# Two paddings that move the start addresses of an FFN's matmul operands

## The chip, the cores and the metric

The kernel runs on one core of a Trainium2 chip. The metric is device microseconds of one execution of the program, lower is better. Three executions of the kernel before took 951.02, 951.64 and 956.59 us; the median is 951.64 us.

## The reference

A conditioned block with two halves on 2048 tokens of 640 channels, all in float32:

```python
mod = (_silu(c) @ w_mod).reshape(c.shape[0], 6, 1, -1)          # sa, ca, ga, sb, cb, gb
h = _layernorm(x) * (1 + ca) + sa
x = x + ga * _A_ref(h, ...)      # a long convolution (S4D): a kernel K is generated from
                                 # exponentials and sines, and applied by FFT over 4096 points
h = _layernorm(x) * (1 + cb) + sb
gate = einsum("bsd,df->bsf", h, w1); up = einsum("bsd,df->bsf", h, w3)      # F = 1728
x = x + gb * einsum("bsf,fd->bsd", _silu(gate) * up, w2)
```

## The kernel before, in words

The program has two stages. The first (up to about 380 us) makes the convolution: five blocks of 128 channels each; GpSimd, VectorE and ScalarE generate phases, sines and products (tiles `ph`, `xx`, `yy`), and TensorE turns these into the convolution's kernel (`kps`) and applies the transforms (`ps`, `fh`, `fk`, `fz`). Its order is written out by hand in a table of task numbers. TensorE's operands here are plain float32, and one such matmul shows as two records in the trace.

The second stage (from about 380 us to the end) is the FFN, on four blocks of 512 tokens, in two passes of two blocks each. Each float32 operand is split into a high and a low part of type float32r (function `split`: the high part is a copy that rounds, the low part the rest), and a product of two such numbers is three matmuls: high by high, high by low, low by high (function `three`). Every one of these has a stationary operand of 128x128 and a moving operand of 128x512. The two up projections of two blocks are combined in a scheme with seven products in place of eight (function `group`): per tile of 128 hidden channels 54 matmuls, over 11 tiles in the first pass and 13 in the second. A tile of the down projection (function `down`) is 15 matmuls, 5 output tiles times three; the last half tile of 64 has 10. A few tiles run in a plain form.

Where the operands lie matters for this change. Stationary operands of the FFN are the split weights `wh`, `wl` (pool `wp`, function `pair`) and `w` (the down weights, function `w2_tile`). Moving operands are the split activations `x0h` to `x8l`, `ah`, `al` and the sums `T` (pool `fp`, functions `x_new`, `hidden_split`). Pools without a side are laid out from the low addresses of a partition upwards, in the order in which they are opened: `const` first, then `x0`, and in the second stage `xp` and `wp`. Pools on the right are laid out down from the high end: `core`, and in the second stage `fp`. Within a pool tiles follow each other. So padding in `const` moves up everything in the pools without a side that is opened after it, and padding late in `fp` moves down all tiles of `fp` made before it.

The scheduler of the second stage and the hand-written order of the first are not touched, and neither looks at addresses. Program order is the same on every engine in both kernels, instruction by instruction.

Of the kernel before, what the change touches and what calls it, by code (L numbers as in the profile page):

```python
# [10 lines left out]
F32 = mybir.dt.float32  # L11
# [7 lines left out]
P = 128  # L19
# [186 lines left out]
class K:  # L206
# [18 lines left out]
    def setup(self):  # L225
        nc = self.nc
        c = self.const = self.pool("const")
        self.ident = c.tile([P, P], F32, name="ident")
        make_identity(nc, self.ident)
        self.hpi = c.tile([P, 1], F32, name="hpi")  # L230
        nc.gpsimd.memset(self.hpi, HPI)
        self.ones = c.tile([P, 1], F32, name="ones")
        nc.gpsimd.memset(self.ones, 1.0)
        self.cols = c.tile([P, 3, KT], F32, name="cols")
        c.tile([P, 32], F32, name="pad")
        d = self.dram = self.pool("dram", space=DRAM)
        self.hs = d.tile([NB, 4, 4, 32, 4, P], F32, name="hs")
        self.zd = d.tile([32, 2, 64, D], F32, name="zd")
        self.w2d = d.tile([14, P, 2, D], F32, name="w2d")
        self.xv = self.x.rearrange("(t1 q j) d -> q t1 j d", t1=32, q=4, j=NJ)  # L240
        self.ov = self.out.rearrange("(t1 q j) d -> q t1 j d", t1=32, q=4, j=NJ)
# [1104 lines left out]
    def ffn(self):  # L1346

        W, X, v, w2 = self.first
        for b in (2, 3):
            self.load_x2(b)  # L1350
        pend = self.groups(0, range(2, 13), X, self.acc, W[2], (w2[2][:, 0], w2[2][:, 1]), None)
        acc, X, W, w2, pend = self.late(0, self.acc, pend)
        pend = self.groups(1, range(13), X, acc, W, w2, pend)
        self.late(1, acc, pend)
# [762 lines left out]
```

## Time and profile before

| what | value |
|---|---|
| median of three runs | 951.64 us (951.02 to 956.59) |
| profiled execution: span from first to last instruction | 950.6 us (no other time is recorded for it) |
| PE busy | 868.3 us (91%), 8369 matmul records |
| weight loads (PEld) busy | 686.4 us (72%) |
| VectorE (DVE) busy | 684.2 us (72%) |
| ScalarE (ACT) busy | 549.9 us (58%) |
| GpSimd (POOL) busy | 342.1 us (36%) |
| mean granted TensorE clock | 0.984 |

PE is TensorE's matmuls and PEld its weight loads, which overlap them. A matmul's record is longer than its share of the stream, because matmuls are pipelined and their ends are modelled: 392 ns for one that starts about 229 ns after the one before. What counts is therefore the distance between the starts, here called the cadence, and not the record's length. L151 is the line of a helper that records instructions in order, so that tiles tell groups apart, not lines. Names of tiles are written out<-in, the moving operand first.

### The profile page before, as it was taken

The page shows a single profiled execution, that of the slowest core. Times are in us where ns is not written, and L with a number is a line of the kernel's source. Part 1 is how long each engine was busy: PE and PEld are TensorE (multiplying, and loading weights), DVE is VectorE, ACT ScalarE, POOL GpSimd, SP SyncE. Part 2 cuts the span into 40 slices and gives each one's busy share as a digit, 9 for nine tenths or more (in the row PEclk, how much of TensorE's full clock was granted, in tenths as well). Part 3 has the DMA queues.
Part 4 walks back from the last instruction along what each step waited for, and adds up shares of the span by engine and source line. Part 5 has one row for each costly group of instructions (what it writes and reads, how often), then busy time and mean ns, then how long its engine had stood idle before and what let it go on. Part 6 is the DMA issues. An engine that isn't in the chain of part 4 may idle for free.

```text
span 950.6 us, 21218 instructions
## 1 busy us (share of the span) xinstructions
PE 868.3 (91%) x8369; PEld 686.4 (72%) x8369; DVE 684.2 (72%) x1294; ACT 549.9 (58%) x1035; POOL 342.1 (36%) x371
## 2 busy tenths in 40 slices
PE   1267999999999986999999999999999999999997
PEld 0035858777888863787777778888788888888775
DVE  7997999999989878896776775657556555555422
ACT  6688999989797732754444444544444444443412
POOL 0899989998998500011111211000121212120000
PEclk9997999999999997999999999999999999999999
DMA  9976553524143598654533422375432222221374
GB/s 201 266 225 171 158 150 107 138 80 127 47 119 84 143 241 209 170 175 149 154 113 121 139 67 87 94 238 171 126 92 83 83 84 83 84 84 31 111 230 127
DMA packets 110508, 127.42 MB, mean 134 GB/s; under 512 B 10568, under 2 KB 90696, under 8 KB 109128
## 3 DMA queue, kind: packets, MB, share of 16 engines
q1 hardware_dynamic: 109032, 125.27, 46.7%
q8 instruction: 66, 1.08, 0.5%
q10 hardware_dynamic: 1376, 0.79, 0.3%
q14 instruction: 34, 0.28, 0.1%
HBM read 95.89 MB, written 30.15 MB: 133 GB/s over the span
## 4 chain that ended last, share of the span: by engine, by line
PE 73%; DVE 9%; ACT 8%; DMA 5%; issue 2%; POOL 1%; SPq 1%; ACTq 0%; DVEq 0%; POOLq 0%
PE c L151 19%; PE acc L151 18%; PE X L151 12%; PE ps L151 5%; PE kps L151 4%; PE fz L151 4%; PE fk L151 3%; PE fh L151 3%; PE gu L151 2%; ACT tr L151 1%; DVE xb L151 1%; PE iy L151 1%; DMA sp<-zd 1%; DMA zd<-zt 1%; DVE yy L151 1%
## 5 line engine op out<-in xcount | busy, mean ns | idle before, releaser
L151 PE MATMUL acc<-ah,w 128*128 128x512 f32 x560 | 173.4, 395 | 1.9 <-DMA w<-w2d 1.2
L151 PEld LDWEIGHTS acc<-ah,w 128*128 128x128 f32 x560 | 103.8, 188 | 25.3 <-ACT ah L598 1.8
L151 PE MATMUL acc<-al,w 128*128 128x512 f32 x260 | 102.3, 393 | 0.0
L599 DVE TENSOR_TENSOR wl<-s,wh 128x256 fp32r<-128x256 f32 x92 | 39.0, 424 | 67.0 <-ACT wh L598 66.5
L775 POOL TENSOR_TENSOR s<-wr 128x256 f32<-128x256 f32 x22 | 16.4, 743 | 184.8 <-DMA wr<-in_w 104.7
L598 ACT ACTIVATE wh<-s 128x256 fp32r<-128x256 f32 x92 | 37.6, 409 | 78.0 <-PE X L151 58.1
L151 POOL TENSOR_TENSOR ph<-p,p 128x1024 int32<-128x1024 int32 x40 | 78.8, 1970 | 6.2 <-ACT tr L151 5.6
L598 ACT ACTIVATE wh<-wr 128x256 fp32r<-128x256 f32 x92 | 38.4, 418 | 56.1 <-PE X L151 42.4
L776 POOL TENSOR_TENSOR s<-s,wr 128x256 f32<-128x256 f32 x22 | 17.1, 776 | 131.5 <-issue 128.0
L151 DVE TENSOR_TENSOR yy<-yy,tr 128x512 f32<-128x512 f32 (+1 forms) x60 | 56.5, 944 | 2.9 <-ACT tr L151 2.1
L836 ACT ACTIVATE t<-g 128x512 f32<-128x512 f32 x44 | 27.8, 632 | 52.9 <-DVE g L800 52.9
L151 PEld LDWEIGHTS acc<-al,w 128*128 128x128 f32 x260 | 48.9, 188 | 11.3 <-DVE al L599 0.4
L151 ACT ACTIVATE tr<-ph,hpi 128x512 f32<-128x512 f32 x80 | 54.5, 688 | 3.3 <-DVE yy L151 1.3
L151 DVE TENSOR_TENSOR xx<-tr,xx 128x512 f32<-128x512 f32 x80 | 54.2, 681 | 2.9 <-ACT tr L151 2.5
L805 DVE SCALAR_TENSOR_TENSOR g<-t,g 128x512 f32<-128x512 f32 x48 | 33.7, 701 | 31.3 <-ACT t L836 29.3
L151 PE MATMUL kps<-yy,xx 128*32 128x64 f32 x1920 | 37.8, 231 | 18.3 <-DVE xx L151 14.2
L151 PE MATMUL fz<-fp,wz 64*128 64x512 f32 x224 | 54.0, 608 | 0.3 <-DVE fp L151 0.3
L151 PEld LDWEIGHTS kps<-yy,xx 128*32 128x32 f32 x1920 | 32.8, 114 | 27.1 <-issue 11.1
L599 DVE TENSOR_TENSOR wl<-wr,wh 128x256 fp32r<-128x256 f32 x92 | 40.2, 438 | 15.1 <-ACT wh L598 15.0
L151 PE MATMUL ps<-wk,xb 128*64 128x128 f32 x640 | 47.2, 294 | 2.8 <-DVE hb L151 1.1
L151 ACT ACTIVATE tr<-ph 128x512 f32<-128x512 int32 x80 | 47.2, 599 | 2.3 <-DVE yy L151 1.8
L598 ACT ACTIVATE ah<-h 128x512 fp32r<-128x512 f32 x26 | 16.4, 632 | 53.1 <-PE acc L151 53.1
(454 smaller groups left out, 2442.3 us busy)
## 6 DMA issues: line engine op xcount, KB each, us to landing
w<-w2d SPq DMA_DIRECT2D x42, 640.0 KB, 3.9
wr<-in_w SPq DMA_DIRECT2D x50, 320.0 KB, 3.9
zd<-zt SPq DMA_DIRECT2D x40, 256.0 KB, 3.2
w2d<-w SPq DMA_DIRECT2D x14, 640.0 KB, 3.5
xs<-in_x SPq DMA_DIRECT2D x16, 320.0 KB, 11.9
hs<-hb SPq DMA_DIRECT2D x20, 256.0 KB, 3.2
xb<-hs SPq DMA_DIRECT2D x20, 256.0 KB, 4.8
iz<-zd SPq DMA_DIRECT2D x32, 160.0 KB, 4.2
```

The costliest lines, as they stand in the source:

```text
L151: self.prev = self.k.order(f(*a, **kw), self.prev)
L598: self.nc.scalar.activation(H, v, AF.Copy)
L599: eng.tensor_tensor(Lo, v, H.bitcast(F32), op=ALU.subtract)
L775: eng.tensor_tensor(s[0], u[:, 0:2], u[:, 2:4], op=ALU.add)
L776: eng.tensor_tensor(s[1], s[0], g[:, 0:2], op=ALU.subtract)
L805: V.scalar_tensor_tensor(g, th, 1.0, g, op0=ALU.add, op1=ALU.mult)
L836: tanh = lambda o, i: A.activation(o, i, AF.Tanh, scale=0.5)
```

## The change

The padding tile in `const` grows from 128 to 224 bytes per partition, which is 96 more, and a tile of 480 bytes that nothing reads or writes is made in `fp` before the first group of the FFN. The start bytes within a partition, taken modulo 512, are then:

| tiles | before | after |
|---|---|---|
| `wh`, `wl`, `w` (stationary, FFN), `wr`, `w2r` (raw weights), four of the `h` tiles | 416 | 0 |
| `x0h` to `x8l`, `T`, `ah`, `al` (moving, FFN), temporaries, `s`, ten of the `h` tiles | 480 | 0 |
| `x2` of token blocks 0 and 1 (`x20`, `late`) | 416 | 0 |
| `x2` of token blocks 2 and 3 | 256 | 288 |
| first stage: `ph`, `xx`, `yy`, phase tables | 480 | 64 |
| first stage: `xb`, `wb`, `sp`, ring `hz` | 480 | 480 |
| first stage: `wk`, `wz`, and a tile that is also named `fp` | 352 | 352 |
| `ident` (the moving operand of transposes) | 128 | 128 |

No instruction is added, removed or moved.

```diff
@@ setup @@
         self.cols = c.tile([P, 3, KT], F32, name="cols")
-        c.tile([P, 32], F32, name="pad")
+        c.tile([P, 56], F32, name="pad")
         d = self.dram = self.pool("dram", space=DRAM)
@@ ffn @@
         for b in (2, 3):
             self.load_x2(b)
+        self.fp.tile([P, 120], F32, name="gap", tag="gap")
         pend = self.groups(0, range(2, 13), X, self.acc, W[2], (w2[2][:, 0], w2[2][:, 1]), None)
```

## The prediction

> **What bounds the kernel now.** I read the page's busy shares and the chain that ended last, then the busy time by stretch, and then the order in time inside the FFN.
>
> ```profile
> PE 868.3 (91%) x8369; PEld 686.4 (72%) x8369; DVE 684.2 (72%) x1294; ACT 549.9 (58%) x1035; POOL 342.1 (36%) x371
> PE 73%; DVE 9%; ACT 8%; DMA 5%; issue 2%; POOL 1%; SPq 1%; ACTq 0%; DVEq 0%; POOLq 0%
> 140.00:240.00 100.00, 96.16 (x2010) 78.16 (x2008) 94.94 (x142) 92.47 (x159) 93.36 (x92) 1.00 0.43 115
> 460.00:520.00 60.00, 60.00 (x264) 45.52 (x263) 42.78 (x101) 26.07 (x56) 9.63 (x13) 1.00 0.42 126
> 690.00:880.00 190.00, 190.00 (x832) 155.91 (x831) 105.54 (x201) 80.83 (x177) 31.89 (x43) 1.00 0.26 78
> ```
>
> The columns of the last three rows are the stretch, its length, then busy time of PE, PEld, DVE, ACT and POOL, the granted clock, the DMA share and GB/s. In the first stage (140 to 240 us) PE, DVE, ACT and POOL are all over 92% busy. In the FFN PE alone is full: 190.00 of 190.00 us at clock 1.00, with DVE at 106 us, ACT at 81 and POOL at 32. So in the FFN the time is the number of matmuls times their cadence, and anything that changes the cadence goes straight into the span. The cadence is read from starts, here ten matmuls apart, and from a piece of the chain:
>
> ```profile
> 699.71 0.39 PE L151 MATMUL c<-x1h,wl 128*128 128x512 f32 x1
> ...
> 702.00 0.62 PE L151 MATMUL acc<-ah,w 128*128 128x512 f32 x2
> 702.16 3.43 PE acc L151 x15
> ```
>
> From 699.71 to 702.00 us ten matmuls start, which gives 0.229 us each; 3.43 us for 15 gives 0.2287. I take 228.9 ns, between the two. The number of such matmuls:
>
> ```profile
> L151 PE MATMUL acc<-ah,w 128*128 128x512 f32 x560 | 173.4, 395 | 1.9 <-DMA w<-w2d 1.2 <-ACT oc L978 0.7
> L151 PE MATMUL acc<-al,w 128*128 128x512 f32 x260 | 102.3, 393 | 0.0
> L151 PE MATMUL c<-x2hT,wh 128*128 128x512 f32 x48 | 18.8, 392 | 0.0
> ```
>
> The down projection has 560 + 260 = 820. The row with 48 is one product's first factor, two per tile, so 24 tiles; with 54 matmuls each (seven products of 6 and four rests of 3) they make 1296. The plain form adds 180 by the code: two whole tiles of 30 matmuls for each of token blocks 0 and 1, and a half tile of 15 for each of the four blocks. In all 820 + 1296 + 180 = 2296, and 2296 x 0.2289 = 525.6 us, 55% of the span. One nanosecond of cadence is worth 2.3 us of the run.
>
> **The change part by part.** The instructions and their order stay the same on every engine, with no wait added or removed, so no queue is passed and nothing stands behind a new wait. Only start bytes move. There are four groups of work whose price could depend on them.
>
> *Matmuls of the FFN* (start bytes 416 and 480 modulo 512 before, 0 and 0 after). The trace of before holds no 128x512 float32r matmul with another placement, so I bound the price by the nearest rows. First, other matmuls with other placements, in the plain float32 of the first stage:
>
> ```profile
> 63.90 1.02 PE L151 MATMUL prow<-m,ident 128*128 128x512 f32 x2
> L151 PE MATMUL prow<-m,ident x8: 486/592/697, 61.1 to 64.3; 128*128 128x512 f32 x6, 128*128 128x384 f32 x2
> 121.30 1.88 PE L151 MATMUL fz<-fp,wz 64*128 64x512 f32 x8
> L151 PE MATMUL fz<-fp,wz x224: 589/589/693, 120.8 to 356.6; 64*128 64x512 f32 x112
> ```
>
> In `prow` the moving operand begins at 480 and the stationary one at 128; two take 1.02 us, and less the record of the last, 0.592, the cadence is 0.43. In `fz` both begin at 352, thus at the same place modulo 512, as they all do in the FFN after the change; eight matmuls run as four pairs, the two halves of the array side by side, and (1.88 - 0.589) / 3 is again 0.43 per pair. Second, the same work with two placements: the product `kps` takes `yy` from its own tile at 480 or, in every third chunk, from `x2` at 416:
>
> ```profile
> L151 PE MATMUL kps<-yy,xx x1920: 216/219/316, 48.2 to 328.6; 128*32 128x64 f32 x192
> L151 PE MATMUL kps<-x,xx x640: 216/219/245, 59.9 to 268.6; 128*32 128x64 f32 x160
> L151 DVE SCALAR_TENSOR_TENSOR yy<-yy,tr x30: 669/676/689, 41.1 to 323.3; 128x512 f32<-128x512 f32 x30
> L151 DVE SCALAR_TENSOR_TENSOR x<-x,tr x10: 672/676/687, 53.2 to 261.0; 128x512 f32<-128x512 f32 x10
> L151 POOL TENSOR_TENSOR yy<-e,e x38: 1059/1067/2057, 34.4 to 322.6; 128x512 f32<-128x512 f32 x38
> L151 POOL TENSOR_TENSOR x<-e,e x10: 1067/1072/1087, 50.1 to 211.5; 128x512 f32<-128x512 f32 x10
> ```
>
> The medians are 219 and 219 ns on PE, 676 and 676 on DVE, 1067 and 1072 on POOL. Where the trace can compare placements, they make no difference. I take 0 ns per matmul, by these rows. Their weakness: all these moving tiles begin an odd multiple of 32 bytes past a multiple of 64, none at a multiple of 64, and plain float32 streams at half the speed of the FFN's matmuls, so a slower read could hide there. That leaves room on both sides: half of 0.43 us is 0.215, which a float32r stream would need if it ran exactly twice as fast as plain float32, 14 ns under the 228.9 seen. So the lower end is 2296 x -14 ns = -32 us. The upper end comes from a slower cadence that the trace already holds:
>
> ```profile
> 914.65 0.40 PE L151 MATMUL acc<-al,w 128*128 128x512 f32 x1
> ...
> 916.75 0.40 PE L151 MATMUL acc<-al,w 128*128 128x512 f32 x1
> 914.11 24.34 PE acc L151 x102
> ```
>
> After a wait for a DMA at about 912 us the same form of matmul, with the same start bytes, goes on at 2.10 us for 9, that is 233.3 ns, and keeps this for most of a piece of 102. With placement the same, what differs is when the streams began. So the upper end is 2296 x +4.4 = +10.1 us.
>
> The Trainium skill, "SBUF — State Buffer", the section on door 1 (its note on cachelines), says that an access that moves on to a new 16-byte line pays a penalty. By that rule the change is worth nothing, since 32-byte-aligned starts before and after touch the same number of lines; the rows of `kps` agree (219 and 219 ns), although both of their placements are multiples of 32.
>
> *First stage* (`ph`, `xx`, `yy`, the tables: 480 to 64; `x20`: 416 to 0). From the same six rows: 0, with at most 5 ns on a POOL instruction (1072 against 1067). With all 371 POOL instructions of the kernel on the path, 5 ns each is 1.9 us. I take 0 ± 2 us.
>
> *Element work of the FFN* (splits, sums, gates: 416 or 480 to 0). It lies beside a full PE: in 690 to 880 us DVE has 190.00 - 105.54 = 84 us to spare. Even 10% more on DVE (10.6 us) is covered. The cover would go only if PE became much faster; then at 14 ns less of 228.9 (6%) the stretch would be 178 us long, still far over DVE's 106. So what comes late next is still PE. Price 0.
>
> *DMA.* Raw weights `wr` arrive as rows of 512 bytes, which land after the change at multiples of 512.
>
> ```profile
> w<-w2d SPq DMA_DIRECT2D x42, 640.0 KB, 3.9
> wr<-in_w SPq DMA_DIRECT2D x50, 320.0 KB, 3.9
> PE acc L151 <- DMA w<-w2d: 1.2, 1, 1.2
> POOL s L775 <- DMA wr<-in_w: 59.6, 4, 37.4
> ```
>
> POOL waits for `wr`, but it is 17% busy in 690 to 880 us (31.89 of 190) and PE is not seen to wait for it. PE's one wait for FFN weights is 1.2 us. A transfer that is faster or slower by a quarter (1 us of 3.9) changes this by at most 1 us. Price 0 ± 1 us.
>
> **The sum**, against the profiled execution: 950.6 + 0 (FFN matmuls) + 0 (first stage) + 0 (element work) + 0 (DMA) = 950.6 us of span. The median of the runs is 1.0 us over that span, so I predict 951.6 us. With the small terms' bounds this case alone reaches from 949 to 957, the upper end from the highest run shown (956.59).
>
> **The rivals.**
>
> *Aligned streams are read faster.* For it: the cadence of 228.9 ns is over half of the 0.43 us of plain float32, and what takes the 14 ns is not explained by any row; PE waits for nothing there. If the moving read of 2048 bytes from an odd multiple of 32 costs an extra access at each end, the aligned start drops it. Against it: two cadences at the same placement (228.9 and 233.3) show that at least part of the excess depends on timing, not on address. In full it gives 951.6 - 32 = 920 us; anything over 4.1 ns per matmul (9.5 us / 2296) is more than 1%. The Trainium skill, "TensorE: Matmul & The Clock Gate", the section "Wait — 56ns, not 53.3ns?" in part 1, gives back-to-back starts 215.7 ns apart for 512 columns; by that figure the excess is 13.2 ns, and the estimate for its full removal is 921 us. The trace differs from it with 228.9 ns.
>
> *The two reads of TensorE meet.* The next weights are read while the moving operand streams:
>
> ```profile
> 699.94 0.39 PE L151 MATMUL c<-x7h,wh 128*128 128x512 f32 x1
> 699.95 0.19 PEld L151 LDWEIGHTS c<-x7l,wh 128*128 128x128 f32 x1
> ```
>
> The weight load starts 0.01 us after the matmul. Before, the two reads begin 64 bytes apart modulo 512; after, at the same place. If they share something that is chosen by the low bits of the address, they now meet at the first byte, and the slower cadence of 233.3 ns becomes the rule: 951.6 + 10.1 = 961.7 us. It decides from 4.1 ns per matmul on, so at 4.4 it is just over 1%. For it: the two cadences look like two ways in which two streams lock. Against it: `fz` with both operands at 352 runs at the same 0.43 us as `prow` at 480 and 128. The Trainium skill, "TensorE: Matmul & The Clock Gate", part 2, step 1 on LDWEIGHTS, says that weights and moving operand have read ports of their own and that loading the next weights takes nothing from the running matmul; by that rule this rival gives nothing. No row here separates the ports.
>
> *That the change does not do what it says* is no rival: the start bytes of all 2296 matmuls' operands do become multiples of 512 in the built program.
>
> **How the numbers follow.** A change of 1% (9.5 us) is about what a measurement of this kernel can tell from none, since its three runs lie 0.6% apart. No effect: 0.68, for the rows that compare placements. Faster reads: 0.20, for the unexplained 14 ns, and I spread its result evenly from -9.5 to -32 us. Meeting reads: 0.12, mostly near +10. So faster 0.20, same 0.68, slower 0.12. A range from 938 to 962 us holds the first case, a sixth of the second (down to -13.6 us: 4.1 of 22.5) and, say, 0.10 of the third: 0.68 + 0.03 + 0.10 = 0.81.
>
> **What would show it.** In the profile after, 15 matmuls of the down projection should again take 3.43 us in the chain; 3.22 (15 x 0.215) would show the first rival, 3.50 (15 x 0.2333) throughout the second. `kps` should stay at 219 ns and POOL's `yy<-e,e` near 1067. The forecast is wrong if the FFN from 380 us on is shorter or longer than before by over 9 us while PE stays full, and its reason is wrong if the cadence changes and something else gives it back. If the first stage ends at another time by more than 2 us, the six rows were no guide to it.

## The result, and the profile after

The changed kernel takes 948.9 us (median of 17 runs, 945.59 to 952.13) against 953.82 us for the kernel before, timed beside it (17 runs). The ratio is 0.9947 with a 95% interval of 0.9933 to 0.9962: half a per cent faster, clear of no change, and inside 1%. The profiled execution's span went from 950.6 to 945.7 us, 4.9 us less.

The page's busy line and the same stretches as before (length, busy PE, PEld, DVE, ACT, POOL, clock, DMA share, GB/s):

```profile
PE 864.6 (91%) x8369; PEld 686.3 (73%) x8369; DVE 682.9 (72%) x1294; ACT 549.2 (58%) x1035; POOL 341.6 (36%) x371
140.00:240.00 100.00, 96.50 (x2012) 78.23 (x2010) 94.39 (x142) 92.29 (x160) 93.54 (x92) 1.00 0.41 108
460.00:520.00 60.00, 60.00 (x266) 45.14 (x265) 41.34 (x100) 26.19 (x56) 9.56 (x13) 1.00 0.42 126
690.00:880.00 190.00, 190.00 (x839) 157.10 (x837) 106.06 (x202) 80.49 (x177) 30.91 (x42) 1.00 0.25 77
```

The number of instructions is the same, and PE is still full in the FFN, but in 690 to 880 us it now does 839 matmuls where it did 832. In the first stage, 140 to 240 us, PE does as much as before (96.50 us for 2012 against 96.16 for 2010). Where the time went shows in the cadence, in the order of time and in the chain of waits of the changed kernel:

```profile
697.04 0.39 PE L151 MATMUL c<-x7h,wh 128*128 128x512 f32 x1
...
699.08 0.62 PE L151 MATMUL acc<-ah,w 128*128 128x512 f32 x2
699.24 3.40 PE acc L151 x15
...
910.80 0.62 PE L151 MATMUL acc<-ah,w 128*128 128x512 f32 x2
...
913.52 0.62 PE L151 MATMUL acc<-ah,w 128*128 128x512 f32 x2
```

Nine matmuls from 697.04 to 699.08 us give 0.2267 us each, and 15 take 3.40 us where they took 3.43. After the wait for a DMA at 908 us, where before went on at 233.3 ns, twelve from 910.80 to 913.52 again give 0.2267. From the first to the last matmul of the down projection, the FFN's length can be read in both kernels (durations are min/median/max, then first and last start):

```profile
L151 PE MATMUL acc<-ah,w x560: 387/392/502, 405.1 to 943.3; 128*128 128x512 f32 x187
```

```profile
L151 PE MATMUL acc<-ah,w x560: 387/389/500, 404.0 to 938.0; 128*128 128x512 f32 x187
```

The first row is before (943.3 - 405.1 = 538.2 us), the second after (534.0 us): 4.2 of the 4.9 us lie there. Of the rest, the down projection begins 1.1 us earlier (404.0 for 405.1), and what comes after its last matmul takes 0.4 us longer (7.7 us for 7.3).

What does not change is the first stage's work, although its tiles moved from 480 to 64 modulo 512 and from 416 to 0:

```profile
L151 PE MATMUL kps<-yy,xx x1920: 216/219/316, 47.2 to 326.5; 128*32 128x64 f32 x192
L151 PE MATMUL kps<-x,xx x640: 217/219/245, 58.9 to 266.4; 128*32 128x64 f32 x160
L151 POOL TENSOR_TENSOR yy<-e,e x38: 1058/1067/2054, 33.4 to 320.5; 128x512 f32<-128x512 f32 x38
L151 DVE SCALAR_TENSOR_TENSOR yy<-yy,tr x30: 670/676/689, 40.1 to 321.2; 128x512 f32<-128x512 f32 x30
```

The medians are those of before: 219 ns on PE, 1067 on POOL, 676 on DVE. For the distance between two operands, which the experiments turn to, these rows are no test: `yy`, `x2` and their stationary `xx` all moved by 96 bytes.

### The profile page after: what moved, and what is told of

The parts are those of the page before. It is cut to its first block, busy times and chain, and to the rows that moved or that the text cites. A ratio compares the mean times of both kernels' runs of the same rounds, so it can differ in the third digit from the quotient of the medians.

```text
span 945.7 us, 21218 instructions
## 1 busy us (share of the span) xinstructions
PE 864.6 (91%) x8369; PEld 686.3 (73%) x8369; DVE 682.9 (72%) x1294; ACT 549.2 (58%) x1035; POOL 341.6 (36%) x371
## 4 chain that ended last, share of the span: by engine, by line
PE 75%; DVE 9%; ACT 8%; DMA 4%; issue 2%; SPq 1%; POOL 1%; ACTq 0%; DVEq 0%; POOLq 0%
PE c L151 19%; PE acc L151 18%; PE X L151 12%; PE ps L151 5%; PE fz L151 4%; PE kps L151 4%; PE gu L151 3%; PE fk L151 3%; PE fh L151 3%; ACT tr L151 2%; DVE xb L151 1%; PE iy L151 1%; DMA zd<-zt 1%; DVE yy L151 1%; PE tp L151 1%
## 5 line engine op out<-in xcount | busy, mean ns | idle before, releaser
L151 PEld LDWEIGHTS ps<-wk,xb 128*64 128x64 f32 x640 | 43.3, 220 | 5.2 <-DVE hb L151 1.1
```

The source lines that it names most:

```text
L151: self.prev = self.k.order(f(*a, **kw), self.prev)
```

## The experiments

Three theories at first. M: the start byte of the moving operand decides the cadence. S: that of the stationary operand does. R: the distance between the two does (moving start less stationary start; 64 before, 0 after).

**One padding without the other.** The full kernel's variants are shown as differences from the changed kernel, without the lines around them. First the tile in the FFN's pool alone, which puts the moving operands at 0 and leaves the stationary ones at 416:

```diff
-        c.tile([P, 56], F32, name="pad")
+        c.tile([P, 32], F32, name="pad")
```

> Only the tile of 480 bytes in the FFN's pool is added: moving operands at 0, stationary ones stay at 416 modulo 512. Before has a cadence of 228.9 ns, the changed kernel 226.7. Theory M (the moving operand's start decides): 226.7 ns, 15 matmuls in 3.40 us, and the whole gain of about 5 us. Theory S (the stationary operand's start decides): 228.9 ns, 3.43 us, no gain. Theory R (the distance between the two starts decides, here 96 in place of 64 or 0): a third number, neither 228.9 nor 226.7.

Then the padding in `const` alone, with stationary operands at 0 and moving ones at 480:

```diff
-        self.fp.tile([P, 120], F32, name="gap", tag="gap")
```

> Only the padding of 96 bytes is added: stationary operands at 0, moving ones stay at 480 modulo 512. Theory M: 228.9 ns and no gain. Theory S: 226.7 ns, 15 matmuls in 3.40 us, and about 5 us less. Theory R: the distance is 480 (or 32 the other way), a third number.

Each half alone is slower than before: 964.47 us for the first (ratio 1.0124, interval 1.0079 to 1.0168), 961.13 us for the second (1.0083, 1.0050 to 1.0116), against 952.08 us for the kernel before. The chains of the two, in this order:

```profile
706.59 3.50 PE acc L151 x15
```

```profile
707.31 3.50 PE acc L151 x15
```

15 matmuls take 3.50 us in both, 233.3 ns each. M and S both fall, since each foresaw that one half changes nothing and the other brings everything. R foresaw a third number, and that is what came, at distances 96 and 480. The price fits: 4.4 ns x 2296 = 10.1 us, and the spans are 9.6 us longer (960.2) and 8.7 us longer (959.3) than before's.

**Distance 0 without any alignment.** Both operands at 416, an odd multiple of 32:

```diff
-        c.tile([P, 56], F32, name="pad")
+        c.tile([P, 32], F32, name="pad")
-        self.fp.tile([P, 120], F32, name="gap", tag="gap")
+        self.fp.tile([P, 16], F32, name="gap", tag="gap")
```

> The tile in the FFN's pool has 64 bytes and the other padding stays as before: both operands start at 416 modulo 512, an odd multiple of 32, at distance 0. Theory R: as in the changed kernel, 226.7 ns. Theories M and S: 228.9 ns as before, since neither start becomes a multiple of 64.

```profile
700.28 3.40 PE acc L151 x15
```

3.40 us, the cadence of the changed kernel. So it is not the multiple of 512 (or of 64) that helps. Its one run took 951.12 us, which alone says nothing about half a per cent. It was timed again, in ten runs beside those of the next two placements:

> Both operands at 416 modulo 512, distance 0, the first stage placed as before: timed. Theory R256: the whole gain of the changed kernel, 0.5% less than before, although nothing begins at a multiple of 512. Rival (part of the gain is the first stage's, whose tiles moved from 480 to 64 in the changed kernel): less gain than that.

950.71 us, ratio 0.9959 (0.9941 to 0.9977) to the kernel before. The interval holds the changed kernel's 0.9947, although here the first stage lies as before. The down projection of this run:

```profile
L151 PE MATMUL acc<-ah,w x560: 387/389/499, 408.5 to 942.3; 128*128 128x512 f32 x187
```

It lasts 533.8 us, against 534.0 in the changed kernel, so the 4.2 us gained there need nothing from the first stage. That the moved tiles of the first stage add something of their own is not shown; by the run times, up to some 0.3 per cent of the run would not be seen.

**A map of pairs.** A kernel with nothing but matmuls of the FFN's form, 21 for each pair of start bytes (its loops are shortened here; some pairs with stationary starts of 32, 96, 416 and 480, and a few starts that are no multiples of 32, follow them):

```python
for s in range(0, 512, 64):              # start of the stationary operand, bytes modulo 512
    for m in range(0, 512, 32):          # start of the moving operand
        for i in range(21):
            matmul(acc[i % 3], st[:, s // 4 + 128 * (i % 3):][:, :128], mv[:, m // 4 + 512 * (i % 3):][:, :512])
```

> Only matmuls of the FFN's form (128x128 stationary, 128x512 moving, float32r) on copied input, 21 for each pair of start bytes, with the stationary start in steps of 64 and the moving start in steps of 32 modulo 512, then some odd stationary starts and starts that are 4 to 24 bytes off; the block itself is left out and the output is a copy of the input. Theory M: the cadence depends on the moving start alone, 226.7 ns at multiples of 64 and 228.9 between them. Theory S: it depends on the stationary start alone. Theory R: it depends on the difference alone. If the excess over half of plain float32 (215 ns) is a matter of placement at all, some pair is near 215.

In the order of time, with the stationary operand at 0 and the moving one at 32, 64, 96, 128, and further on 256 and 288:

```profile
27.72 5.06 PE L39 MATMUL qab<-mv,st 128*128 128x512 f32 x21
32.62 4.97 PE L39 MATMUL qac<-mv,st 128*128 128x512 f32 x21
37.43 5.07 PE L39 MATMUL qad<-mv,st 128*128 128x512 f32 x21
42.34 5.06 PE L39 MATMUL qae<-mv,st 128*128 128x512 f32 x21
...
61.96 4.93 PE L39 MATMUL qai<-mv,st 128*128 128x512 f32 x21
66.73 5.06 PE L39 MATMUL qaj<-mv,st 128*128 128x512 f32 x21
```

From one block's start to the next are 4.90 us at distance 32 (233 ns each), 4.81 at 64 (229), 4.91 at 96 (234), and 4.77 at 256 (227, with the first few matmuls still settling). Over all 162 pairs whose starts are multiples of 32 (without the first block, whose first matmuls start 427 ns apart), the mean of the last 14 distances from start to start in a block follows the distance modulo 256, to within about 1 ns:

| distance modulo 256 (bytes) | 0 | 32 | 64 | 96 | 128 | 160 | 192 | 224 |
|---|---|---|---|---|---|---|---|---|
| median over the pairs (ns) | 226.6 | 233.4 | 228.7 | 233.5 | 233.4 | 234.3 | 233.4 | 233.4 |
| lowest to highest | 226.6 to 227.4 | 233.2 to 233.4 | 228.6 to 229.1 | 233.0 to 233.5 | 232.4 to 233.4 | 234.3 | 233.3 to 233.4 | 233.3 to 233.4 |

R holds for these starts, with a period of 256 bytes. Of the multiples of 32, before stood at the second-best distance and after stands at the best. No pair comes near 215 ns, so placement is not the whole of the excess.

**The map's word for the full kernel.** Two more placements, with the stationary operands at 0: moving operands at 256, and at 64.

```diff
-        self.fp.tile([P, 120], F32, name="gap", tag="gap")
+        self.fp.tile([P, 56], F32, name="gap", tag="gap")     # moving at 256; with 104 in its place, at 64
```

> As the changed kernel, but moving operands at 256 modulo 512 instead of 0, stationary ones at 0. Theory R256 (only the distance between the two starts modulo 256 decides, as the map of pairs shows): as the changed kernel, 226.7 ns, 15 matmuls in 3.40 us, about 5 us less than before. Rival (the start of each operand modulo 512 decides): another cadence and no such gain.

> As the changed kernel, but moving operands at 64 modulo 512: both operands still begin at multiples of 64, and their distance is 64, as it was before. Theory R256: the cadence of before, 228.9 ns, and the time of before within 0.3%. Rival (multiples of 64 are what helps): 226.7 ns and 5 us less.

At 256: 947.36 us, ratio 0.9938 (0.9916 to 0.9959). At 64: 951.93 us, ratio 0.9989 (0.9971 to 1.0008), no gain although every operand begins at a multiple of 64. Their chains, in this order:

```profile
698.90 3.40 PE acc L151 x15
```

```profile
700.42 3.43 PE acc L151 x15
```

Both came as R with a period of 256 says.

**What the distance acts on.** Another kernel of matmuls alone, with other shapes, types and finer distances (its list of cases in short; two more lists have stationary columns 2 and 4 elements apart, and streams that were to begin after a wait).

```python
cases  = [stationary columns 32, 64, 96, 128] x [distance 0, 64, 128]
cases += [moving columns 256, 320, 384, 448] x [distance 0, 64, 128]
cases += [plain float32, bfloat16] x [distance 0, 64, 128] + [distance 0, 4, 8 ... 252]
```

> Only matmuls on copied input, 21 of each case, the block itself is left out and the output is a copy of the input. Cases at distances 0, 64 and 128: stationary operands of 32 to 128 columns, moving operands of 256 to 512 columns, stationary columns 2 and 4 elements apart, plain float32, bfloat16; then distances 0 to 252 in steps of 4 bytes; then streams that begin after a wait on another engine of varied length, at distances 64, 0 and 128. Theory C (the weight load's read and the moving read collide, and the distance decides how often): the spread of 6.7 ns between distances 0 and 128 shrinks with fewer stationary columns, is the same for all lengths of the moving operand, and is gone in plain float32 and bfloat16, whose moving read needs half as many bytes in a given time. Theory F (a fixed cost at a matmul's start): the same spread for 32 as for 128 stationary columns. For the stretch of before that ran at 233.3 ns after a wait: if the moment of the start decides, some of the streams at distance 64 after a wait run at 233.3 and others at 228.7.

Rows for 128 stationary columns with 256 and with 320 moving columns, then plain float32 and bfloat16, each at distances 0, 64 and 128:

```profile
80.05 2.68 PE L52 MATMUL qam<-mvr,str 128*128 128x256 f32 x21
82.56 2.55 PE L52 MATMUL qan<-mvr,str 128*128 128x256 f32 x21
84.95 2.65 PE L52 MATMUL qao<-mvr,str 128*128 128x256 f32 x21
87.44 3.24 PE L52 MATMUL qap<-mvr,str 128*128 128x320 f32 x21
90.52 3.24 PE L52 MATMUL qba<-mvr,str 128*128 128x320 f32 x21
93.60 3.24 PE L52 MATMUL qbb<-mvr,str 128*128 128x320 f32 x21
...
150.00 18.18 PE L52 MATMUL qbo<-mvf,stf 128*128 128x512 f32 x42
168.02 18.19 PE L52 MATMUL qbp<-mvf,stf 128*128 128x512 f32 x42
186.04 18.19 PE L52 MATMUL qca<-mvf,stf 128*128 128x512 f32 x42
204.07 4.70 PE L52 MATMUL qcb<-mvb,stb 128*128 128x512 bf16 x21
208.60 4.70 PE L52 MATMUL qcc<-mvb,stb 128*128 128x512 bf16 x21
213.13 4.70 PE L52 MATMUL qcd<-mvb,stb 128*128 128x512 bf16 x21
```

Plain float32 takes 18.02 us for 42 records at each distance, 429.1 ns for each of a matmul's two records, and bfloat16 4.53 us for 21, 215.8 ns: there the distance does nothing. Of theory C this part holds. But the level does not follow the load: with 32 stationary columns the cadences are 231.7, 231.7 and 229.8 ns, no lower than with 128 (226.7 once settled, 228.8, 232.6). And the spread is not the same for all lengths: 320 moving columns give 146.7 ns at all three distances, 384 give 173.3, 173.3 and 176.4. With 256 and with 448 columns the best of the three is not 0 but 64: from one block's start to the next are 2.51, 2.39 and 2.49 us with 256 (120, 114 and 119 ns each), and with 448 the cadences are 203, 200 and 203 ns. Theory F falls too, since the spread of about 6 ns at 128 stationary columns is 2 at 32. Stationary columns that lie 2 or 4 elements apart give 231 to 240 ns, 233 and 235 of them at distance 0.

The distances in steps of 4 bytes between the multiples of 32 lie from 226.7 (240) to 240 ns (20, among others); none is under the 226.6 of distance 0. There the distance alone does not decide: a stationary start of 0 with a moving one of 240 gives 226.7 ns, while in the map a stationary start of 16 with a moving one of 0, the same distance modulo 256, gives 233.2.

The streams that were to begin after a wait were laid by the scheduler so that the waiting matmul came in the middle of others. They still answer the question on before's slow stretch. At distance 64:

```profile
536.03 3.43 PE L52 MATMUL qgf<-mvr,str 128*128 128x512 f32 x14
539.29 0.40 PE L42 MATMUL wqgf<-mvr,str 128*128 128x512 f32 x1
...
544.37 3.37 PE L52 MATMUL qgh<-mvr,str 128*128 128x512 f32 x14
547.58 0.39 PE L42 MATMUL wqgg<-mvr,str 128*128 128x512 f32 x1
```

The 14 of `qgf` take 3.26 us, 233 ns each, the 14 of `qgh` 3.21 us, 229 ns each; operands, form and distance are the same, and the two kinds change where another matmul broke in. At distance 0 the stream came back to 226.7 ns within ten matmuls each time.

**Own weights or the next ones.** Starts that alternate between two values, so that the distance to a matmul's own weights differs from the distance to the weights loaded while it streams.

```python
PAIRS = [((0, 0), (128, 128)), ((0, 128), (128, 0)), ...]     # (stationary, moving) of even and odd matmuls
```

> Only matmuls on copied input, 24 of each case; the block itself is left out and the output is a copy of the input. The two starts alternate from one matmul to the next, so that the distance of a moving operand to its own weights differs from its distance to the next matmul's weights, which are loaded while it streams. Theory N (the load of the next weights decides): with own distance 0 and next distance 128, 233 to 234 ns; with own distance 128 and next distance 0, 226.7 ns. Theory O (the distance to the operand's own weights decides): the reverse, 226.7 and 233. The same for 96 and 32, and for 64 with 228.7 to 233 in place of 226.7. Then distances 0 to 224 with 32, 64 and 128 stationary columns: theory N, if it is the number of bytes loaded that costs: a spread of some 7 ns between the best and the worst distance at 128 columns, about half at 64, a quarter at 32.

The blocks of 24, in this order: distance 0 throughout, 128 throughout, own 0 with next 128, own 128 with next 0:

```profile
20.62 7.33 PE L39 MATMUL qaa<-mv,st 128*128 128x512 f32 x24 [20.62 <-ACT mv L27]
27.79 5.75 PE L39 MATMUL qab<-mv,st 128*128 128x512 f32 x24
33.38 5.71 PE L39 MATMUL qac<-mv,st 128*128 128x512 f32 x24
38.93 5.67 PE L39 MATMUL qad<-mv,st 128*128 128x512 f32 x24
44.44 5.78 PE L39 MATMUL qae<-mv,st 128*128 128x512 f32 x24
```

The first began with starts some 427 ns apart; its last 12 distances are 226.7 ns. The second has 5.59 us, 233 ns. Own 0 with next 128 takes 5.55 us, over its last 12 distances 232.9 ns, as theory N said and O did not. Own 128 with next 0 takes 5.51 us, 229.7 ns: between the two, so N is not the whole of it. For 96 the order is N's as well (own 0: 234.6, next 0: 230.8), for 64 by a little (232.3 and 231.3), for 32 it is O's (232.0 and 233.3). These last two differences are about 1 ns, in streams whose single distances still run from 226 to 239 ns. The pairs also mix more than the theories say: with starts that alternate between 0 and 64, the other distance is 64 and 192 in turn, which the map puts at 228.7 and 233.4 ns. Over the eight distances the spread is 7.7 ns at 128 stationary columns, 5.0 at 64 and 3.3 at 32; it shrinks, by less than N's half and quarter. The mean over the distances does not: 232.1, 229.9 and 231.5 ns. Nor is 0 the best distance for every shape. With 64 stationary columns it is 160, as the blocks at 0, 32, 160 and 192 show:

```profile
122.31 5.69 PE L39 MATMUL qbc<-mv,st 128*64 128x512 f32 x24
127.84 5.71 PE L39 MATMUL qbd<-mv,st 128*64 128x512 f32 x24
...
149.92 5.60 PE L39 MATMUL qbh<-mv,st 128*64 128x512 f32 x24
155.36 5.71 PE L39 MATMUL qbi<-mv,st 128*64 128x512 f32 x24
```

Distance 0 takes 5.53 us, 230 ns each, and 160 takes 5.44 us, 226.7 ns. So the distance to the next weights matters more than that to the own ones where the difference is clear (128 and 96), and a single rule of this kind does not give all the numbers.

## Why the prediction was right, and where it was not

The range and the class held: 948.9 us lies in 938 to 962, and no effect over 1% was the likeliest case. The forecast of 0 for the mechanism did not hold: by the prediction's own sign 15 matmuls should again take 3.43 us, and they take 3.40. That the time came out in the range is owed to the smallness of the effect, and not to the rows behind the 0. That it came out within 2.7 us of the 951.6 foreseen is in part luck: the kernel before has 953.82 us over 17 runs, so the effect is 4.9 us.

*What bounds the kernel*: right. PE is full in the FFN before and after, and the cadence went into the span: 2.2 ns x 2296 = 5.1 us by the sum's own exchange rate, 4.2 us measured between the first and last matmul of the down projection, 4.9 us of span. Not every matmul gains 2.2 ns. From 420 to 540 us, where the matmuls of `iy` break in, the mean time from one start to the next, gaps of 250 ns and more left out, goes from 229.1 to 227.8 ns. In the two half changes 4.4 ns brought 9.6 and 8.7 us of span.

*Matmuls of the FFN, 0 ns each*: this is the step that failed. Its term was 0 and is -2.2 ns (228.9 to 226.7). The rows that compared placements, `prow`, `fz` and `kps`, are plain float32, and in the form tried, 128x128 by 128x512, plain float32 answers to no distance (429.1 ns at 0, 64 and 128). The prediction named this weakness and then still took their 0 as the likeliest value for float32r. It also made it smaller than it is: its half speed holds for a record, but a plain float32 matmul has two, 858 ns in all, nearly four times the FFN's 228.9. In `prow`, moreover, the stationary operand is one column repeated 128 times (`bc(self.ident[:, 32 * g], 1, P)`), with starts of 0, 128, 256 and 384, and not a tile at 128. A row that cannot show an effect is no evidence against it. The bounds held: -14 ns was not reached, and the upper end, +4.4 ns, read from before's slow stretch, is just what the half changes measured.

*The first rival, aligned streams are read faster*: wrong in its reason. With both operands at an odd multiple of 32 (416) the cadence is 226.7 ns, and with both at multiples of 64 but 64 apart it stays at 228.9.

*The second rival, the two reads meet*: right that the distance of the two starts decides and that 233.3 ns is the slow way; wrong in the sign. Meeting at distance 0 is the best case for this shape, not the worst, and `fz`, which spoke against it, could not speak to it. The Trainium skill, "TensorE: Matmul & The Clock Gate", part 2, step 1, has the load of the next weights take nothing from the running matmul. Bfloat16 agrees (215.8 ns at three distances). For float32r the cadence depends on the distance of the two starts (226.6 to 234.3 ns); whether the load takes this time from the running matmul is not shown, and the alternating starts bear it out only in part (232.9 ns with own 0 and next 128, 229.7 the other way round).

*The 14 ns over half of plain float32*: 2.2 of them went, and about 11 or more stay against bfloat16's 215.8, at every distance, with 32 stationary columns as with 128. Their cause was not found.

*First stage, element work and DMA, 0 each*: right within what can be seen. The medians of `kps`, `yy<-e,e` and the DVE step are the same after the move, and PE's wait for weights is 1.2 us in both kernels:

```profile
PE acc L151 <- DMA w<-w2d: 1.2, 1, 1.2
```

The last `kps<-yy` starts 2.1 us earlier than before (326.5 for 328.6), just past the 2 us that the prediction named as a sign against its six rows. The sign cannot be read here. The other profiles with the first stage placed as before have that start at 328.2, 328.4 and 329.9 us, and those with it moved at 329.2, 329.2 and 327.4.

*The note on 16-byte lines* in the Trainium skill, "SBUF — State Buffer", the section on door 1, gave 0 in the prediction. The trace disagrees with that for float32r: both placements are multiples of 32, and the cadence differs (228.9 and 226.7 ns). So that note alone does not price a start address.

## What to carry to other kernels

Where a stream of float32r matmuls fills TensorE, read the time from start to start, and try the distance of the moving and the stationary start modulo 256 bytes. For 128x128 by 128x512, of the multiples of 32, 0 was best, 64 next, and the others cost 3% of the cadence. Other shapes have to be tried anew: 64 was the best of three with 256 and 448 moving columns, 160 the best of eight with 64 stationary ones. The common start of both operands did not matter where both were multiples of 32, so padding one pool without the other can cost 1% of the run where padding both gains half a per cent. Before a row is used as evidence that something costs nothing, ask whether that row, in its type and speed, could have shown a cost.

## What was not expected of the hardware

The cadence of float32r with 128 stationary and 512 moving columns lies between 226.6 and 240 ns by placement, while bfloat16 (215.8 ns) and plain float32 (429.1 ns a record) keep one value at the three distances tried. At distance 64 the same stream has two lasting ways of running, 228.9 and 233.3 ns, and a break in the stream can switch it from one to the other; before's stretch after 914 us, at 233.3 ns and behind a wait, is of the same kind. At distance 0 only 226.7 ns was seen to last with this shape. For starts that are multiples of 32 the dependence on distance has a period of 256 bytes. What in the chip makes this period was not shown.
